# Loading the later x blocks of an attention and gated-MLP kernel through GpSimd's DMA queue

## The chip, the cores and the metric

The kernel runs on one core of a Trainium2 chip. The metric is the device time of one execution in microseconds (us), and the median of several executions is compared. A core has a matrix engine (TensorE, PE in the profile), three engines for elementwise work (VectorE DVE, ScalarE ACT, GpSimd POOL), a fifth, SyncE (SP), which here only issues transfers, and 16 DMA engines that move data between the chip's main memory (DRAM) and the on-chip memory. Each of the five engines has a queue of instructions of its own and works through it in order.

## The reference

For 2048 tokens of width 576, all in float32:

```python
xn = layernorm(x)                       # x: 1 x 2048 x 576
q, k, v = split(xn @ wqkv)              # 32 heads of 18
s = softmax(q @ k.T * 18**-0.5) @ v     # per head, over all 2048 keys
s = concat_heads(s) @ wo
gate = xn @ W_gate                      # 576 x 4608
h = where(gate > 0, gate, 0) * (xn @ W_up)
g = silu(h @ W_down)                    # 4608 x 576
out = x + s * g
```

## The kernel before

Every float32 product is made of three products of a high and a low part of its operands, so each operand is first split in two ("split", by GpSimd for the weights).

*First stage.* The 2048 tokens are normalized and transposed in four groups g of 512 tokens. Each group's x becomes nine chunks of 64 features (KC = 9), high and low part, and is kept as a tile `x` of 128 rows: rows 0 to 63 and rows 64 to 127 hold the same kind of chunk for the two row halves of TensorE. The groups are also written to DRAM as `xTd`, and q, k and v are made from them and written to DRAM (`qd`, `kd`, `vd`).

*Main stage.* 144 units (numbered k in the code), 36 for each group of 512 tokens. Unit k = 36 g + f makes 128 of the 4608 hidden features for group g: `up(k)` issues 54 matmuls `pg<-x,gw` (27 for each row half, three for each chunk of x, chunk 0 first), woven together with matmuls of attention (`pm` for the maxima of the scores, `psx` for the scores). After an odd unit TensorE does 64 matmuls `po` of attention, after an even one the down projections `py` of the two units before, which read `hh` (h, split) and `dw` (W_down, split).

*The x tiles.* There are eleven buffers (`xA`, KC + 2), nine of them in use. A takeover to the next group therefore runs like this: in `up(k)` of the last unit but one of a group (f = NF - 2, k = 34, 70 and 106), `load_x` is called for chunks 0 and 1 of the next group, into the two free buffers; in the last unit (k = 35, 71 and 107), after each chunk c of the old group has been read, `load_x` is called for chunk c + 2 of the new one. Each `load_x` issues two transfers of 64 rows x 4 KB (256 KB). So there are 4 and then 14 transfers at each of three takeovers; the first group is loaded in the same way at the end of the first stage.

*What sets the order.* The order on TensorE, VectorE and GpSimd is that of the code (kept by `pinned`, `mm`, `vec` and `gp`); the transfers on SyncE are partly kept in the code's order and partly ordered by a scheduler. A transfer on SyncE or GpSimd waits in its queue for the buffer to be free and for one of eight semaphores that the queue's transfers take in turn, so for the landing of the transfer eight before it; what is behind it in the queue waits too. The x loads have their own issuing line, L299 in the profile. GpSimd's other instructions all carry L85, and most of SyncE's L97, since helpers record them. On GpSimd stand, for each unit: the split of the next unit's weights `gw<-rg`, the split of `dw<-rd`, the low part of `hh`, and some adds into `y`.

Of the kernel before, what the change touches and what calls it, by code (L numbers as in the profile page):

```python
# [19 lines left out]
def kernel(  # L20
# [10 lines left out]
    nc = tc.nc  # L31
# [129 lines left out]
    def xtile(pl):  # L161
        return pl.tile([P, 2, 512], F32R, tag="x", name="x")
# [132 lines left out]
    def load_x(g, c):  # L295
        xc = xtile(xA)
        for t in range(2):
            pinned(
                nc.sync.dma_start(  # L299
                    xc[t * R : (t + 1) * R].rearrange("p a s -> p (a s)").bitcast(F32),  # L300
                    xTd[g, c // 2, c % 2 * R : c % 2 * R + R],
                )
            )
        xcur.setdefault(g, []).append(xc)

    with ExitStack() as st:
# [293 lines left out]
        for g in range(NQ):  # L600
# [64 lines left out]
            else:  # L665
                for j in range(4):
                    v_job(wv, g, j)
                    if j == 0 and g == 0:
                        nxt = load_rows(g + 2)
                    if j == 1:  # L670
                        spill(g, marks[-1] if g == 0 else None)
                    if j and g == NQ - 2:
                        for c in range(3 * j - 3, 3 * j):
                            load_x(0, c)
# [24 lines left out]
    def up(k):  # L699

        g, f = units[k]
        gw = gus.pop(k)
        if k < N1 and (k % 2 == 0 or k == N1 - 1):
            ps = [psO.tile([P, 512], F32, name="po"), shared("pg2")]
        else:
            ps = [bank("pg0"), bank("pg1")]
        last = f == NF - 1 and k + 1 < len(units)
        if f == NF - 2 and k + 2 < len(units):
            for c in range(2):
                load_x(units[k + 2][0], c)  # L710
        xg = xcur[g]

        def ops(t, c, i, j, rows):
            return gw[rows, i, c, :], xg[c][rows, j, :]

        def half(t):
            for n, _ in enumerate(row_half(ps[t], ops, t)):
                c = n // len(PRODUCTS)
                if t and last and n % len(PRODUCTS) == 2 and c + 2 < KC:
                    load_x(units[k + 1][0], c + 2)  # L720
                    if c == KC - 3:
                        load_up(k + 2)
                yield

        return ps, [half(t) for t in range(2)]
# [439 lines left out]
```

## Time and profile before

| | |
|---|---|
| median of 3 runs | 2573.6 us (2573.19 to 2574.91) |
| the profiled execution | 2572.87 us |
| its span | 2571.1 us |
| PE, busy | 2564.9 us |
| DVE, ACT, POOL, busy | 1847.1, 1474.5, 1274.7 us |
| transfers x<-xTd | 72, of 256 KB each, all on SyncE's queue |

The span reaches from the first to the last instruction of the profiled execution; the 1.8 us between it and that execution's time lie around it. Busy times of different engines lie beside each other and don't add up. Positions such as 681.18 are us from the span's start.

### The profile page before, as it was taken

The page shows a single profiled execution, that of the slowest core. Times are in us where ns is not written, and L with a number is a line of the kernel's source. Part 1 is how long each engine was busy: PE and PEld are TensorE (multiplying, and loading weights), DVE is VectorE, ACT ScalarE, POOL GpSimd, SP SyncE. Part 2 cuts the span into 40 slices and gives each one's busy share as a digit, 9 for nine tenths or more (in the row PEclk, how much of TensorE's full clock was granted, in tenths as well). Part 3 has the DMA queues.
Part 4 walks back from the last instruction along what each step waited for, and adds up shares of the span by engine and source line. Part 5 has one row for each costly group of instructions (what it writes and reads, how often), then busy time and mean ns, then how long its engine had stood idle before and what let it go on. Part 6 is the DMA issues. An engine that isn't in the chain of part 4 may idle for free.

```text
span 2571.1 us, 61531 instructions
## 1 busy us (share of the span) xinstructions
PE 2564.9 (100%) x25301; PEld 2035.3 (79%) x25301; DVE 1847.1 (72%) x3019; ACT 1474.5 (57%) x3005; POOL 1274.7 (50%) x1003
## 2 busy tenths in 40 slices
PE   9999999999999999999999999999999999999999
PEld 8899987777777777777777777777777777777788
DVE  6336677777877778877777777887777877778125
ACT  3222146666666666666666666666666666666652
POOL 5246764444464444444464444444445444444554
PEclk9999999999999999999999999999999999999999
DMA  8965432323543223222363322332354232222246
GB/s 255 298 205 134 103 86 47 85 68 81 125 112 71 72 70 72 64 71 70 93 145 81 74 71 69 73 77 58 80 130 108 69 79 69 70 62 59 68 137 200
DMA packets 263833, 254.60 MB, mean 99 GB/s; under 512 B 27648, under 2 KB 208640, under 8 KB 263552
## 3 DMA queue, kind: packets, MB, share of 16 engines
q1 hardware_dynamic: 255808, 223.01, 34.9%
q0 software_dynamic: 7744, 27.66, 3.2%
q8 instruction: 199, 3.26, 0.6%
q14 instruction: 82, 0.67, 0.1%
HBM read 203.54 MB, written 46.53 MB: 97 GB/s over the span
## 4 chain that ended last, share of the span: by engine, by line
PE 98%; DVE 1%; POOL 0%; issue 0%; DMA 0%; ACT 0%; POOLq 0%; ACTq 0%
PE pg L68 34%; PE po L68 18%; PE py L68 18%; PE pm L68 10%; PE psx L68 10%; PE pq L68 3%; PE pw L68 2%; PE pv L68 2%; PE tps L76 0%; PE warm L76 0%; DMA qd<-hh 0%; POOL gw L85 0%; DVE hh L129 0%; POOL kd L85 0%; POOL kq L85 0%
## 5 line engine op out<-in xcount | busy, mean ns | idle before, releaser
L268 DVE TENSOR_REDUCE mx<-pm 128x1 f32<-128x512 f32 x2048 | 1371.6, 690 | 355.7 <-PE pm L68 283.7
L68 PE MATMUL pg<-x,gw 64*128 64x512 f32 x7533 | 1359.3, 392 | 0.0
L97 ACT ACTIVATE p<-psx 128x512 f32<-128x512 f32 x2048 | 1097.8, 604 | 203.1 <-PE psx L68 162.7
L68 PEld LDWEIGHTS pg<-x,gw 64*128 64x128 f32 x7533 | 1027.4, 186 | 84.5 <-issue 1.8
L85 POOL TENSOR_TENSOR hh<-h,hh 128x512 fp32r<-128x512 f32 x144 | 185.3, 1287 | 810.1 <-ACT hh L740 810.0
L68 PE MATMUL py<-dw,hh 64*128 64x288 f32 x6912 | 477.7, 292 | 0.0
L68 PEld LDWEIGHTS py<-dw,hh 64*128 64x128 f32 x6912 | 472.8, 184 | 5.8 <-ACT h L97 0.6
L68 PE MATMUL po<-p,va 128*32 128x512 f32 x4096 | 452.7, 594 | 0.0
L68 PEld LDWEIGHTS po<-p,va 128*32 128x32 f32 x4096 | 126.5, 110 | 291.3 <-issue 280.1
L85 POOL TENSOR_TENSOR gw<-rg,gw 128x1152 fp32r<-128x1152 f32 x131 | 349.9, 2671 | 10.5
L790 DVE TENSOR_TENSOR y<-py,y 128x288 f32<-128x288 f32 x422 | 171.7, 452 | 139.7 <-PE py L68 139.6
L68 PE MATMUL psx<-qT,kq 56*128 56x512 f32 x608 | 231.0, 392 | 0.0
L68 PE MATMUL pm<-kq,qT 54*128 54x512 f32 x608 | 226.0, 396 | 0.0
L85 POOL TENSOR_TENSOR dw<-rd,dw 128x576 fp32r<-128x576 f32 x144 | 206.1, 1432 | 11.5
L68 PE MATMUL psx<-kq,kA 56*128 56x512 f32 x512 | 195.2, 393 | 0.0
L68 PE MATMUL psx<-kq 56*128 56x512 f32 x512 | 195.0, 393 | 0.0
L68 PE MATMUL pm<-kA,kq 54*128 54x512 f32 x512 | 191.7, 397 | 0.3 <-DVE mx L268 0.3
L68 PE MATMUL pm<-kq 54*128 54x512 f32 x512 | 191.3, 397 | 0.0
L774 ACT ACTIVATE mark<-ident 128x1 f32<-128x1 f32 x288 | 58.4, 203 | 219.2 <-PE py L68 219.0
L85 POOL CAST gw<-rg 128x1152 fp32r<-128x1152 f32 x131 | 153.8, 1174 | 57.3 <-DMA rg<-in_B_W_up_dram 51.0
L85 POOL TENSOR_TENSOR y<-add,y 128x576 f32<-128x576 f32 x61 | 87.3, 1431 | 186.3 <-ACT add L97 180.8
L740 ACT ACTIVATE hh<-h 128x512 fp32r<-128x512 f32 x144 | 90.8, 631 | 123.2 <-DVE h L733 123.2
(106 smaller groups left out, 2543.1 us busy)
## 6 DMA issues: line engine op xcount, KB each, us to landing
rd<-in_B_W_down_dram SPq DMA_DIRECT2D x144, 288.0 KB
rg<-in_B_W_gate_dram SPq DMA_DIRECT2D x131, 288.0 KB
rg<-in_B_W_up_dram SPq DMA_DIRECT2D x131, 288.0 KB
x<-xTd SPq DMA_DIRECT2D x72, 256.0 KB
qd<-hh POOLq DMA_DIRECT2D x16, 512.0 KB, 4.2
kd<-hh POOLq DMA_DIRECT2D x16, 512.0 KB, 5.7
xTd<-x SPq DMA_DIRECT2D x16, 512.0 KB
kq<-kd SPq DMA_DIRECT2D x210, 36.0 KB
```

What stands on the lines that cost most here:

```text
L68: return tc.keep_in_program_order(nc.tensor.matmul(*args, **kw))
L85: return lambda *args, **kw: tc.keep_in_program_order(op(*args, **kw))
L97: i = op(*args, **kw)
L268: vec(nc.vector.tensor_reduce(mx[:, h, b, j, c : c + 1], ps, axis=AX.X, op=ALU.max))
L740: copy = nc.scalar.activation(hhs[k][:, 0], h, AF.Copy)
L774: seen.append(pinned(nc.scalar.activation(mark, ident[:, :1], AF.Copy)))
L790: vec(nc.vector.tensor_tensor(ys[j][:, cs], outs_[m], ys[j][:, cs], ALU.add))
```

## The change

The x tiles of the first group are still issued by SyncE; those of the second, third and fourth group (g = 1, 2, 3) are issued by GpSimd.

```diff
@@ load_x(g, c)
         xc = xtile(xA)
         for t in range(2):
             pinned(
-                nc.sync.dma_start(
+                (nc.gpsimd if g else nc.sync).dma_start(
                     xc[t * R : (t + 1) * R].rearrange("p a s -> p (a s)").bitcast(F32),
                     xTd[g, c // 2, c % 2 * R : c % 2 * R + R],
                 )
```

54 of the 72 transfers change their queue. The orders on TensorE, VectorE and ScalarE stay as they are. Three places at the first takeover (units 34 to 36) show what moves; the other two takeovers have the same pattern.

GpSimd, units 34 and 35, after the change (`hh`, `gw`, `dw` and `y` are as above, `rg` and `rd` are the weights as loaded):

```order
L85 TENSOR_TENSOR gw<-rg,gw 128x1152
L299 DMA x<-xTd 64x1024 x4
L85 TENSOR_TENSOR hh<-h,hh 128x512
L85 TENSOR_TENSOR y<-add,y 128x576
L85 CAST dw<-rd 128x576
L85 TENSOR_TENSOR dw<-rd,dw 128x576
L85 CAST gw<-rg 128x1152
L85 TENSOR_TENSOR gw<-rg,gw 128x1152
L85 CAST dw<-rd 128x576
L85 TENSOR_TENSOR dw<-rd,dw 128x576
L299 DMA x<-xTd 64x1024 x14
L85 TENSOR_TENSOR hh<-h,hh 128x512
```

Before, the same rows stood there without the two of L299. The four transfers now stand between the split of unit 35's weights and hh of unit 34, the fourteen between the split of dw and hh of unit 35.

SyncE at the same place, before (`od<-on` writes attention's results, `kq<-qd` and `kA<-kd` load strips of q and k, `qT<-nr` the negated maxima):

```order
L97 DMA od<-on 18x512 x2
L299 DMA x<-xTd 64x1024 x4
L97 DMA rd<-in_B_W_down_dram 128x576
L299 DMA x<-xTd 64x1024 x14
L97 DMA rg<-in_B_W_gate_dram 64x9x128
L97 DMA rg<-in_B_W_up_dram 64x9x128
L97 DMA rd<-in_B_W_down_dram 128x576
L97 DMA kq<-qd 18x1024 x2
L97 DMA rg<-in_B_W_gate_dram 64x9x128
L97 DMA rg<-in_B_W_up_dram 64x9x128
```

and now:

```order
L97 DMA od<-on 18x512 x2
L97 DMA rd<-in_B_W_down_dram 128x576
L97 DMA rg<-in_B_W_gate_dram 64x9x128
L97 DMA rg<-in_B_W_up_dram 64x9x128
L97 DMA rd<-in_B_W_down_dram 128x576
L97 DMA kq<-qd 18x1024 x6
L97 DMA rg<-in_B_W_gate_dram 64x9x128
L97 DMA rg<-in_B_W_up_dram 64x9x128
```

The weights and the second rd no longer stand behind the x loads, and all six strips of q go together ahead of the following weights. At the second takeover six strips of k and the tile `va` of v move up in the same way.

TensorE, the end of unit 36's pg, where the last chunk (x_10348) is first read; the order is the same, and the two waits are now for GpSimd's transfers (DMASW) where they were for SyncE's (DMAHW). Before:

```order
L68 MATMUL pg0_10454<-x_10326,gw_10206 128x512
L68 MATMUL pg1_10455<-x_10348,gw_10206 128x512 [waits DMAHW0_49]
L68 MATMUL pg0_10454<-x_10348,gw_10206 128x512 [waits DMAHW7_49]
L68 MATMUL pg1_10455<-x_10348,gw_10206 128x512
L68 MATMUL pg0_10454<-x_10348,gw_10206 128x512
```

and now:

```order
L68 MATMUL pg0_10454<-x_10326,gw_10206 128x512
L68 MATMUL pg1_10455<-x_10348,gw_10206 128x512 [waits DMASW1_49]
L68 MATMUL pg0_10454<-x_10348,gw_10206 128x512 [waits DMASW0_49]
L68 MATMUL pg1_10455<-x_10348,gw_10206 128x512
L68 MATMUL pg0_10454<-x_10348,gw_10206 128x512
```

Each chunk has such a pair of waits, one for each row half.

## The prediction

> **What bounds the kernel now.** I read the page first: busy time, then the chain that ended last.
>
> ```profile
> span 2571.1 us, 61531 instructions
> PE 2564.9 (100%) x25301; PEld 2035.3 (79%) x25301; DVE 1847.1 (72%) x3019; ACT 1474.5 (57%) x3005; POOL 1274.7 (50%) x1003
> PE 98%; DVE 1%; POOL 0%; issue 0%; DMA 0%; ACT 0%; POOLq 0%; ACTq 0%
> ```
>
> TensorE is busy for 2564.9 of 2571.1 us and carries 98% of the chain. Its work is not touched, so the change can win at most the 6.2 us in which TensorE is idle in the whole span, and it loses whatever TensorE is made to wait. The question is only whether x still arrives in time. The execution that was profiled took 2572.87 us, 0.7 below the median of the runs, 2573.6; I make the sum as a difference and add it to the median.
>
> Next I read SyncE's queue in order of time where the second 512 tokens take over (units 34 to 36, k in the code). Columns: start, duration, instruction, count.
>
> ```profile
> 663.92 2.40 SPq L299 DMA_DIRECT2D x<-xTd  x4
> 680.72 0.36 SPq L97 DMA_DIRECT2D rd<-in_B_W_down_dram  x1
> 681.18 10.30 SPq L299 DMA_DIRECT2D x<-xTd  x14
> 692.22 0.63 SPq L97 DMA_DIRECT2D rg<-in_B_W_gate_dram  x1
> ```
>
> Four transfers (chunks 0 and 1) go early into free buffers. The other fourteen (chunks 2 to 8) go from 681.18 on, each pair when unit 35 has read a chunk for the last time; the next weights, rg, stand behind them. GpSimd in the same stretch, with its idle time before an instruction in brackets:
>
> ```profile
> 658.96 2.66 POOL L85 TENSOR_TENSOR gw<-rg,gw 128x1152 fp32r<-128x1152 f32 x1
> 672.76 1.28 POOL L85 TENSOR_TENSOR hh<-h,hh 128x512 fp32r<-128x512 f32 x1 [11.13 <-ACT hh L740]
> ...
> 685.23 1.43 POOL L85 TENSOR_TENSOR dw<-rd,dw 128x576 fp32r<-128x576 f32 x1
> 689.19 1.28 POOL L85 TENSOR_TENSOR hh<-h,hh 128x512 fp32r<-128x512 f32 x1 [2.53 <-ACT hh L740]
> 704.17 1.15 POOL L85 CAST gw<-rg 128x1152 fp32r<-128x1152 f32 x1 [13.70 <-DMA rg<-in_B_W_up_dram]
> ```
>
> GpSimd has the time. But its queue is in order, and the fourteen now stand behind the dw split, which ends at 685.23 + 1.43 = 686.66. Then TensorE, where unit 36, the first on the new tokens, stands:
>
> ```profile
> 686.28 7.07 PE L68 MATMUL po<-p,va 128*32 128x512 f32 x64
> 693.29 0.50 PE L68 MATMUL pg<-x,gw 64*128 64x512 f32 x1
> ...
> 702.26 0.64 PE L68 MATMUL pg<-x,gw 64*128 64x512 f32 x4
> 702.74 0.62 PE L68 MATMUL pg<-x,gw 64*128 64x512 f32 x3
> ```
>
> Unit 36 begins at 693.29. Its last six pg matmuls read chunk 8 and start at about 702.26; each chunk is read some 1.1 us after the one before. Last, the rate of the transfers (columns: stretch, length, busy time and count of PE, PEld, DVE, ACT, POOL, granted clock, DMA share, GB/s):
>
> ```profile
> 682.00:698.00 16.00, 16.00 (x142) 9.44 (x140) 10.52 (x18) 9.36 (x17) 5.86 (x4) 1.00 1.01 242
> 1290.00:1305.00 15.00, 15.00 (x134) 8.67 (x132) 9.55 (x16) 8.38 (x16) 4.94 (x4) 1.00 1.04 237
> 1897.00:1912.00 15.00, 15.00 (x134) 8.35 (x132) 9.51 (x17) 8.38 (x16) 5.09 (x4) 1.00 1.00 238
> ```
>
> In all three takeovers x moves at 237 to 242 GB/s with the DMA engines' share at 1.00 to 1.04. Fourteen transfers of 256 KB are 3.67 MB, so 15.2 to 15.5 us; before, they and the rd of 0.295 MB were through by about 681.18 + 0.8 + 3.96/0.242 = 698.4. TensorE needs two chunks in 2.2 us while a chunk takes 2.2 us to arrive, so the last chunk decides, with a slack of about 3 us after its landing.
>
> **The change part by part.** *Four early transfers.* They go at 658.96 + 2.66 = 661.62, into an idle time of 11.13 us. GpSimd's own issues in the trace, then the issue line of its 512 KB stores (KB, median us to landing), then a stretch in which little but such stores moves:
>
> ```profile
> 160.22 0.61 POOL L85 DMA_DIRECT2D qd<-hh  x1 [4.83 <-DVE hh L129]
> ...
> 162.02 0.60 POOL L85 DMA_DIRECT2D kd<-hh  x1
> ```
>
> ```profile
> qd<-hh POOLq DMA_DIRECT2D x16, 512.0 KB, 4.2
> ```
>
> ```profile
> 186.00:190.00 4.00, 3.91 (x51) 3.61 (x53) 3.64 (x7) 0.72 (x2) 3.92 (x3) 1.00 0.72 266
> ```
>
> The four issues around 160 move 256 KB each, as x does, at 0.61 us: 4 x 0.61 = 2.4 us, covered by the 11.13. Cost 0; without that cover hh would be 2.4 us late, and down projections read it much later.
>
> *Fourteen late transfers.* They start 686.66 - 681.18 = 5.48 us later than on SyncE, which is more than the slack. A 512 KB store lands 4.2 us after its issue (the issue line), of which 0.524/0.266 = 2.0 us are its bytes at the rate of the last row; so 2.2 us lie before and behind them. Chunk 8 lands at 686.66 + 2.2 + 15.2 = 704.1, if nothing else moves. Issue at 0.61 each would be done in 8.5 us and does not pace it. TensorE waits 704.1 - 702.26 = 1.8 us. The same for the third and fourth 512 tokens, from the end of dw and the activation h that ends the unit (at 703.46 here, 1.2 behind the first read of chunk 8):
>
> ```profile
> 703.46 0.60 ACT L97 ACTIVATE h<-pg 128x512 f32<-128x512 f32 x1 [0.35 <-PE pg L68]
> 1292.31 1.43 POOL L85 TENSOR_TENSOR dw<-rd,dw 128x576 fp32r<-128x576 f32 x1
> 1310.52 0.60 ACT L97 ACTIVATE h<-pg 128x512 f32<-128x512 f32 x1 [0.36 <-PE pg L68]
> 1899.47 1.43 POOL L85 TENSOR_TENSOR dw<-rd,dw 128x576 fp32r<-128x576 f32 x1
> 1917.68 0.60 ACT L97 ACTIVATE h<-pg 128x512 f32<-128x512 f32 x1 [0.36 <-PE pg L68]
> ```
>
> 1293.74 + 2.2 + 15.5 - 1309.32 = 2.1 us, and 1900.90 + 2.2 + 15.4 - 1916.48 = 2.0 us. Sum of the lower ends: 5.9 us.
>
> *SyncE's queue runs ahead.* With x gone from it, rg goes when gw is split (684.5), and rd and six strips of q go from 686.7 on, beside x instead of behind it; for the third 512 tokens also six strips of k and the tile va. That is new competition:
>
> ```profile
> rd<-in_B_W_down_dram SPq DMA_DIRECT2D x144, 288.0 KB
> kq<-qd SPq DMA_DIRECT2D x96, 72.0 KB
> kA<-kd SPq DMA_DIRECT2D x174, 36.0 KB
> va<-vd SPq DMA_DIRECT2D x16, 320.0 KB
> ```
>
> ```profile
> 717.60:719.60 2.00, 2.00 (x20) 1.68 (x18) 1.90 (x4) 1.89 (x4) 0.63 (x1) 1.00 0.47 127
> ```
>
> The last row is a stretch in which almost only such strips move: 127 GB/s, on about half of the engines. At most x loses rd 0.295/0.242 = 1.2 us and q 6 x 0.074/0.127 = 3.5 us at each takeover, 4.7; at the second also k 0.221/0.127 = 1.7 and va 0.328/0.242 = 1.4. Together 3 x 4.7 + 3.1 = 17.2 us; at least 0, if they fit beside x. The share of 1.01 says full; but these engines reached 415 GB/s in another stretch (row below), so 242 is not all they can do. I take half, 8.6 us.
>
> *GpSimd held up.* The issues wait for landings (one of eight semaphores each), so the last goes out when the sixth has landed, about 686.66 + 2.2 + 6 x 1.08 + 1 = 696 to 698. Then come hh of unit 35 (1.28 us; TensorE needs it 0.4 us into the py that follow unit 36) and gw of unit 37 (3.85 us, done by about 703; before, it started at 704.17 after waiting 13.70 for rg). Both earlier than needed: cost 0. If the cover went, hh would be late next. That rg comes sooner wins nothing, since TensorE did not wait for it.
>
> Sum: 5.9 + 8.6 = 14.5 us, with ends at 5.9 and 23.1. 2573.6 + 14.5 = 2588.1 us.
>
> *A rule against this.* The rate of GpSimd's queue for this load is in no row; the fastest stretch I found is SyncE storing 128-partition tiles:
>
> ```profile
> 64.00:67.00 3.00, 3.00 (x30) 2.72 (x28) 0.28 (x1) 0.20 (x1) 0.76 (x1) 1.00 1.03 415
> ```
>
> The Trainium skill's "DMA: Bandwidth & Descriptors", section "Anatomy of one DMA", fits a transfer from GpSimd as about 2.0 us plus its bytes at 436 GB/s. As an estimate by that page, the fourteen would land at 686.66 + 2.0 + 8.4 = 697.1 and TensorE would not wait at all: sum 0, the first rival. Against it, the Trainium skill's "SBUF — State Buffer", section "Door 1: The DMA port swizzle", says that 64 partitions reach only half of the ports; the 242 GB/s agree, and x still moves 64 partitions at a time.
>
> **The rivals.** *x arrives in time after all* (not slower): GpSimd's queue moves x faster, say because both halves of a chunk overlap better. It decides at the rate that moves 3.67 + 0.295 MB between 686.66 + 1.1 = 687.8 (half of the 2.2 on each side) and 702.26 - 1.1 = 701.2: 3.96/13.4 = 296 GB/s. For it speaks the 415; against it three stretches at 237 to 242 for this very transfer, and GpSimd's stores at 266. Then nothing is lost: 2573.6, at most 1 us off.
> *GpSimd keeps only two transfers in flight* (its queue too short): 7 x (2.2 + 2.16) = 30.5 us instead of 15.2, 15 us more at each takeover, 2588.1 + 45 = 2633. Against it: the four issues around 160 went out back to back at 0.6 us each with none landed.
> *Faster*: SyncE's freed queue takes waits off TensorE. It has 6.2 us of idle time in the whole span, and none in the stretches above, where its busy time is the full 16.00 and 15.00 us; 2568 at best.
>
> **How the numbers follow.** From no change, 0.2% is 5.1 us, about what a measurement of this kernel can tell. The forecast (late x, sum between the ends 5.9 and 23.1) has 0.75; x in time, or nearly so, 0.16; two in flight 0.05; faster 0.03; the remaining 0.01 goes with slower, for mishaps. Slower therefore 0.81, same 0.16, faster 0.03. The forecast's own range is 2579.5 to 2596.7. The range reaches down to 2575, into the case of x nearly in time, and up to 2598; it leaves out the two in flight and most of no wait at all.
>
> **What would show it.** The three groups of fourteen x issues on GpSimd start right behind dw at 686.7, 1293.7 + w and 1900.9 + w, where w is the delay gathered so far, and take 9 to 11 us each. TensorE waits for x three times, in pieces of about 1 us at the last chunks of units 36, 72 and 108, 3 to 8 us in each; the matmul counts and their mean times stay. The cast of gw no longer waits 13.7 us for rg. Fewer than 2 us of waits at each takeover would mean a faster queue or free competition; waits at py for hh or pg for gw, that GpSimd was held longer than I think.

## The result and the profile after

The changed kernel takes 2601.35 us (median of 5 runs, 2600.62 to 2602.84) against 2573.65 for the kernel before: 27.7 us more, ratio 1.0108 (95% interval 1.0097 to 1.012). It is slower, as forecast; the size, 14.5 us, was about half of what came, and 2601.35 lies above the range's end of 2598. The profiled execution of the changed kernel took 2601.35 us, its span is 2599.6.

The page, for the rows that answer to those of before:

```profile
span 2599.6 us, 61558 instructions
PE 2578.6 (99%) x25301; PEld 2040.9 (79%) x25301; DVE 1853.2 (71%) x3019; ACT 1475.7 (57%) x3005; POOL 1301.7 (50%) x1057
PE 96%; DMA 2%; DVE 1%; POOL 0%; issue 0%; ACT 0%; POOLq 0%; ACTq 0%
L68 PE MATMUL pg<-x,gw 64*128 64x512 f32 x7533 | 1371.7, 394 | 14.2 <-DMA x<-xTd 13.8
x<-xTd POOLq DMA_DIRECT2D x54, 256.0 KB, 9.8
```

TensorE's work is the same 25301 matmuls. Of the 28.5 us by which the span grew, 14.8 are idle time of TensorE (21.0 us now, 6.2 before) and 13.7 are more busy time (2578.6 against 2564.9). Before, the matmuls `pg<-x,gw` never waited:

```profile
L68 PE MATMUL pg<-x,gw 64*128 64x512 f32 x7533 | 1359.3, 392 | 0.0
```

Now TensorE sits idle 14.2 us ahead of them, 13.8 of these for x. The last row of the page has the 54 transfers of x, now on GpSimd's queue, with a median of 9.8 us from issue to landing.

The first takeover in order of time: SyncE's queue, then GpSimd's.

```profile
681.05 0.36 SPq L97 DMA_DIRECT2D rd<-in_B_W_down_dram  x1
684.91 0.60 SPq L97 DMA_DIRECT2D rg<-in_B_W_gate_dram  x1
685.56 0.63 SPq L97 DMA_DIRECT2D rg<-in_B_W_up_dram  x1
687.02 0.36 SPq L97 DMA_DIRECT2D rd<-in_B_W_down_dram  x1
687.44 2.83 SPq L97 DMA_DIRECT2D kq<-qd  x6
709.85 0.60 SPq L97 DMA_DIRECT2D rg<-in_B_W_gate_dram  x1
```

```profile
685.57 1.42 POOL L85 TENSOR_TENSOR dw<-rd,dw 128x576 fp32r<-128x576 f32 x1
686.94 4.10 POOL L299 DMA_DIRECT2D x<-xTd  x8
694.57 0.52 POOL L299 DMA_DIRECT2D x<-xTd  x1 [3.53 <-PE psx L68]
...
704.19 0.52 POOL L299 DMA_DIRECT2D x<-xTd  x1 [0.29 <-DMA x<-xTd]
704.72 1.29 POOL L85 TENSOR_TENSOR hh<-h,hh 128x512 fp32r<-128x512 f32 x1
705.95 1.14 POOL L85 CAST gw<-rg 128x1152 fp32r<-128x1152 f32 x1
```

The fourteen start right behind the dw split, as worked out (686.94 against 686.66). Ahead of x and beside it SyncE now sends rg, rd and six strips of q, which stood behind x before. Eight issues go out at once; the other six wait, five of them for a landing of x by these rows (the profile puts the first of the six down to a `psx` matmul), so the last leaves at 704.19. TensorE's weight loads that waited for x, with the wait in brackets, and the down projections that follow:

```profile
696.56 0.18 PEld L68 LDWEIGHTS pg<-x,gw 64*128 64x128 f32 x1 [0.56 <-DMA x<-xTd]
701.50 0.18 PEld L68 LDWEIGHTS pg<-x,gw 64*128 64x128 f32 x1 [4.17 <-DMA x<-xTd]
703.95 0.28 PEld L68 LDWEIGHTS pg<-x,gw 64*128 64x128 f32 x1 [0.80 <-DMA x<-xTd]
...
709.72 0.18 PEld L68 LDWEIGHTS pg<-x,gw 64*128 64x128 f32 x1 [1.03 <-DMA x<-xTd]
711.83 2.29 PEld L68 LDWEIGHTS py<-dw,hh 64*128 64x128 f32 x32
```

From here on a takeover is judged by its *lateness*: how much further the down projections `py` behind the first unit of the new tokens stand from a `po` group five units earlier (the one behind unit 31, at the first takeover) than they did before. For the first takeover the `po` rows (chain of waits, before and after) and the `py` row of before are

```profile
619.02 7.00 PE po L68 x64
```

```profile
619.32 7.00 PE po L68 x64
```

```profile
703.22 2.94 PEld L68 LDWEIGHTS py<-dw,hh 64*128 64x128 f32 x42
```

(711.83 - 619.32) - (703.22 - 619.02) = 8.31 us. In the same way the second takeover gives (1330.68 - 1234.75) - (1310.27 - 1226.10) = 11.76 and the third (1945.26 - 1853.65) - (1917.44 - 1833.25) = 7.42. The three make 27.5 of the 28.5 us of span. The waits alone don't: grouped over the run they are

```profile
PEld pg L68 <- DMA x<-xTd: 22.7, 18, 4.2
PE pg L68 <- DMA x<-xTd: 13.8, 9, 3.7
```

What is missing is in TensorE's clock, by stretch (length, busy time and count of PE, PEld, DVE, ACT, POOL, granted clock, DMA share, GB/s):

```profile
690.00:698.00 8.00, 7.64 (x65) 3.62 (x57) 3.40 (x5) 3.58 (x7) 2.07 (x5) 1.00 1.05 221
698.00:701.00 3.00, 0.00 (x0) 0.00 (x0) 0.05 (x1) 0.38 (x1) 0.52 (x1) 1.00 1.03 227
701.00:706.00 5.00, 4.32 (x20) 2.65 (x20) 1.93 (x3) 1.86 (x4) 2.83 (x5) 0.66 1.00 243
706.00:711.00 5.00, 3.94 (x30) 2.75 (x32) 2.64 (x5) 3.51 (x6) 4.14 (x5) 1.00 0.40 120
```

After the 4 us gap the granted clock is 0.66 on the mean of 5 us (0.50 in the middle), so matmuls count as busy for longer. The last wait, at 709.72, ends with a landing of x when the clock is back at 1.00: here x sets the end, and the slow clock fills time that would have been a wait.

### The profile page after: what moved, and what is told of

The parts are those of the page before. It is cut to its first block, busy times and chain, and to the rows that moved or that the text cites. A ratio compares the mean times of both kernels' runs of the same rounds, so it can differ in the third digit from the quotient of the medians.

```text
span 2599.6 us, 61558 instructions
## 1 busy us (share of the span) xinstructions
PE 2578.6 (99%) x25301; PEld 2040.9 (79%) x25301; DVE 1853.2 (71%) x3019; ACT 1475.7 (57%) x3005; POOL 1301.7 (50%) x1057
## 3 DMA queue, kind: packets, MB, share of 16 engines
q1 hardware_dynamic: 251488, 208.85, 32.5%
## 4 chain that ended last, share of the span: by engine, by line
PE 96%; DMA 2%; DVE 1%; POOL 0%; issue 0%; ACT 0%; POOLq 0%; ACTq 0%
PE pg L68 33%; PE py L68 18%; PE po L68 17%; PE pm L68 10%; PE psx L68 9%; PE pq L68 4%; DMA x<-xTd 2%; PE pw L68 2%; PE pv L68 2%; PE tps L76 0%; PE warm L76 0%; POOL dw L85 0%; POOL x L299 0%; DVE wqk L638 0%; DVE hh L129 0%
## 5 line engine op out<-in xcount | busy, mean ns | idle before, releaser
L68 PE MATMUL pg<-x,gw 64*128 64x512 f32 x7533 | 1371.7, 394 | 14.2 <-DMA x<-xTd 13.8
L85 POOL TENSOR_TENSOR dw<-rd,dw 128x576 fp32r<-128x576 f32 x144 | 205.9, 1430 | 11.5
```

The source lines that it names most:

```text
L68: return tc.keep_in_program_order(nc.tensor.matmul(*args, **kw))
L85: return lambda *args, **kw: tc.keep_in_program_order(op(*args, **kw))
```

## The experiments

Three readings of the loss were set against each other. *Shared*: one set of DMA engines serves both queues, and x is late by its place behind the dw split and by all that SyncE now sends ahead of it. *Queue*: GpSimd's queue moves x more slowly by itself. *Clock*: TensorE's slow stretches are the loss. The table has each run's three latenesses, from its own `po` and `py` rows as above, its median and its ratio to the kernel before (2573.6 to 2573.8 beside it). The latenesses are from one profiled execution each, and executions of one run lie up to 5 us apart (2592.10 to 2596.75 in pool_all_held, of which the slowest was profiled), and how much of that lies in the latenesses is not known, so a difference of a few us between two sums is safe only where it shows at each takeover.

| run | lateness at the three takeovers, us | sum | median, us | ratio (95%) |
|---|---|---|---|---|
| changed kernel | 8.3, 11.8, 7.4 | 27.5 | 2601.35 | 1.0108 (1.0097 to 1.012) |
| early_only | 0.0, 0.0, 0.0 | 0.0 | 2573.64 | 0.9999 (0.999 to 1.0008) |
| pool_all_held | 2.8, 3.1, 3.0 | 8.9 | 2593.18 | 1.008 (1.0064 to 1.0095) |
| pool_strips_held | 4.6, 6.1, 4.8 | 15.4 | 2589.05 | 1.0059 (1.0044 to 1.0074) |
| pool_weights_held | 3.7, 7.2, 3.8 | 14.7 | 2592.11 | 1.0069 (1.0053 to 1.0086) |
| sync_held | 3.6, 4.5, 3.7 | 11.8 | 2589.1 | 1.0061 (1.0046 to 1.0076) |
| sync_weights_first | 5.6, 5.1, 6.5 | 17.2 | 2590.54 | 1.0066 (1.0049 to 1.0083) |
| x_first | 4.0, 2.1, 5.1 (gw, not x) | 11.2 | 2582.88 | 1.0038 (1.0023 to 1.0053) |
| strips_beside | 5.7, 8.7, 6.3 | 20.6 | 2601.28 | 1.0107 (1.0092 to 1.0122) |
| weights_beside | 6.9, 7.3, 6.7 | 20.8 | 2595.49 | 1.0084 (1.0069 to 1.0099) |
| all_beside | 11.9, 13.8, 11.5 | 37.1 | 2610.35 | 1.014 (1.0123 to 1.0157) |

**early_only**: of the kernel before, only the four early transfers go to GpSimd.

```diff
-                nc.sync.dma_start(
+                (nc.gpsimd if g and c < 2 else nc.sync).dma_start(
```

> The kernel before with only the four early x transfers of each block (chunks 0 and 1) through GpSimd, and the fourteen late ones through SyncE. The prediction's term for the early four is nothing: 2573.6 us (2572.5 to 2575). Queue: the same, as they are issued some 25 us before they are needed. A loss here would show that the early part had a price.

No loss. All of it is in the fourteen late transfers.

**pool_all_held**: the changed kernel, with the transfers that ran ahead held back. `hold[0]` is the last x transfer of a takeover, from its issue until unit f = 3 of the new tokens; `after(i, j)` lets i wait for the end of j. Each of rg, rd ("w"), the q and k strips and va ("s") passes through `hold_back`.

```diff
+    HELD = 'ws'
...
+    def hold_back(i, kind):
+        if hold[0] is not None and kind in HELD:
+            after(i, hold[0])
...
-            sp.dma_start(rds[k], wd[f * P : (f + 1) * P, :])
+            hold_back(sp.dma_start(rds[k], wd[f * P : (f + 1) * P, :]), "w")
```

> The changed kernel, x through GpSimd, with one addition: SyncE's transfers that ran ahead at a takeover (rg, rd, the q and k strips, va) wait until the last of the sixteen x transfers has landed. Shared: only the later place of x is left, about 2579.5 us (2577 to 2583). Queue: GpSimd's queue is as slow as before, so about 2600 us (above 2595).

(The last of the x transfers is the fourteenth, not the sixteenth.) The total missed both ranges. The lateness points to *shared*: 8.9 of the 27.5 us are left, so 18.6 came from what SyncE sent. The queues by themselves, in the kernel before, in this one, and in the changed one, each over a stretch full of x (packets, MB, share of the 16 engines; q1 is SyncE's queue, q0 GpSimd's):

```profile
DMA packets 996, 3.30 MB, mean 236 GB/s; under 512 B 195, under 2 KB 195, under 8 KB 993
q1 hardware_dynamic: 993, 3.27, 101.7%
```

```profile
DMA packets 993, 3.26 MB, mean 233 GB/s; under 512 B 202, under 2 KB 202, under 8 KB 990
q0 software_dynamic: 990, 3.23, 103.5%
```

```profile
DMA packets 720, 2.21 MB, mean 221 GB/s; under 512 B 157, under 2 KB 157, under 8 KB 718
q0 software_dynamic: 484, 1.61, 75.9%
q1 hardware_dynamic: 234, 0.58, 27.1%
```

Alone, GpSimd's queue moved 3.23 MB in 14 us (690 to 704), SyncE's 3.27 in 14 us (684 to 698): 231 and 234 GB/s, the same packets filling the same engines. In the changed kernel (690 to 700) x got 1.61 MB in 10 us, 161 GB/s, because SyncE's packets took 27.1% of the engines' time. That falsifies *queue* and shows *shared*. The Trainium skill's "DMA: Bandwidth & Descriptors", section "Queues, rings and completion order", says that each DMA engine takes turns between the queues that have work for it. The trace agrees in so far as both queues had their part of the same engines, 75.9% and 27.1%; the turns themselves it does not show.

The total was worse than expected because the held rg came late in its turn (SyncE's issue of rg, then GpSimd's cast of gw):

```profile
706.32 0.60 SPq L97 DMA_DIRECT2D rg<-in_B_W_gate_dram  x1
```

```profile
711.92 1.15 POOL L85 CAST gw<-rg 128x1152 fp32r<-128x1152 f32 x1 [12.39 <-DMA rg<-in_B_W_up_dram]
```

TensorE then waited for gw (1.64 us at 715.84) and for ScalarE's `p` behind the `py`, which the expectation had left out. So for runs that hold something back the lateness, not the total, tells what x lost.

**pool_strips_held** and **pool_weights_held**: the same with `HELD = 's'` and `HELD = 'w'`.

> The changed kernel, with only the q and k strips and va of a takeover held until the last x transfer has landed; rg and rd still run ahead. Shared: the later place (2 us) and rg and rd (some 2.7 us) are left at each of three takeovers, about 2588 us (2585 to 2591). Queue: about 2600 us.

> The changed kernel, with only rg and rd of a takeover held until the last x transfer has landed; the q and k strips and va still run ahead. Shared: the later place (2 us), the strips (3.5 us) and at the second takeover k and va (3 us) are left, about 2593 us (2589 to 2596). Queue: about 2600 us.

Both came near *shared* and 8 to 12 us below *queue*. For pool_weights_held that is in part luck: its parts had promised 19.5 us of lateness, 14.7 came, and the held rg, late in its turn, added about 6 elsewhere. And measured so, the pieces do not add up: over the 8.9 of the place, rg and rd cost 6.5 and the strips with va 5.8, and 6.3 of the 27.5 are missing. The three runs at the end are on that.

**sync_held** and **sync_weights_first**: GpSimd issues no x. In the first, SyncE's late x waits for the dw split, GpSimd's place; in the second, rg and rd are put ahead of x. The lines with `kept` keep these transfers in the code's order.

```diff
+            if g and c == 2 and t == 0:
+                after(ld, dw_end[0])
...
+                        kept, sp.kept = sp.kept, True
                         load_up(k + 2)
+                        sp.kept = kept
```

```diff
-                    if c == KC - 3:
-                        load_up(k + 2)
...
+        if units[k][1] == NF - 1 and k + 1 < len(units):
+            kept, sp.kept = sp.kept, True
+            load_up(k + 2)
+            load_down(k + 1)
+            sp.kept = kept
```

> SyncE issues every x again, as before the change, but its first of the fourteen late x transfers of a takeover waits until GpSimd has ended the last dw split, which is where GpSimd's queue has them; rg and rd stay behind x. Theory "shared" (one set of DMA engines; x is late by its place and by what SyncE now sends ahead of it): only the later place is left, about 2 us at each of three takeovers as the prediction worked out, so about 2579.5 us. Rival "queue" (GpSimd's queue moves x more slowly by itself): the queue's share of the 27.7 us is gone and the place's is left, again some 6 us, so about 2579.5 too; but if the late start itself were the cause, this run would stand near 2601. Rival "clock" (the granted TensorE clock drops after a gap and that drop is most of the loss): with small gaps no drop, 2579 or less.

> The kernel before, all x through SyncE, with the takeover's rg and rd transfers put ahead of the fourteen late x transfers in SyncE's queue; GpSimd issues no x. Shared: x is late by the time that rg and rd take on the DMA engines, and by what SyncE waits for a free rg buffer: 3 to 5 us a takeover, 2583 to 2588 us. Queue: SyncE's queue is fast, x at most 2 us late, 2574 to 2579.5 us.

Without GpSimd's queue the same loss appears: 11.8 us of lateness from the place alone (8.9 on GpSimd) and 17.2 with rg and rd ahead (15.4 for place, rg and rd on GpSimd). Both totals are above their forecasts, by some 10 and by 2.5 us. That SyncE's runs come out later does not show a better queue: in sync_held rg, rd and two strips follow x so closely (699.40 to 704.17) that they run beside its last part, and in pool_all_held nothing does. Of the 17.3 us by which sync_held's span is longer than before, 5.5 lie outside the three latenesses; TensorE's waits for ScalarE's `p` grew there by 3.1 us over the run (4.8 against 1.7), and the rest stays open.

**x_first**: the changed kernel, but in the last unit of a group GpSimd issues the fourteen ahead of its gw and dw splits.

```diff
                     if c == KC - 3:
+                        split_up(k + 1)
+                        split_down(k)
                         load_up(k + 2)
...
+        early_split = k >= len(units) - 1 or units[k][1] < NF - 1
+        if early_split:
+            split_up(k + 1)
...
+            if k in rds and early_split:
                 split_down(k)
```

> The changed kernel, but in the last unit of a block of 512 tokens GpSimd issues the fourteen x transfers ahead of its splits of gw and dw (both splits moved behind them, ahead of the next rg load), so that x starts as soon as its buffers come free, ahead of what SyncE sends. Shared: x has the engines almost alone again and lands in time, about 2573.6 us (2572 to 2577; the splits of gw and dw come some us later and are needed later still). Queue: the same transfers by the same queue, still late by the queue's slowness, 2580 us or more.

x was in time: all waits of TensorE for it come to 0.3 us over the three takeovers, with the strips still running beside it. So the queue can do the job from the old place, at least where rg comes behind x (at 696.86). The total, 2582.88, missed *shared* and lies where *queue* had put it, but for another reason: gw is needed right at the takeover, not later as the expectation assumed. TensorE's waits for gw at the first and second takeover, and the six us that hold each wait and the six after (columns as above):

```profile
696.89 0.19 PEld L68 LDWEIGHTS pg<-x,gw 64*128 64x128 f32 x2 [2.00 <-POOL gw L85]
1307.38 0.19 PEld L68 LDWEIGHTS pg<-x,gw 64*128 64x128 f32 x2 [2.01 <-POOL gw L85]
```

```profile
692.00:698.00 6.00, 4.42 (x35) 2.02 (x29) 1.03 (x2) 1.30 (x3) 5.53 (x6) 1.00 1.06 227
698.00:704.00 6.00, 6.00 (x42) 4.93 (x40) 4.23 (x7) 4.47 (x9) 2.19 (x2) 0.72 1.07 231
...
1303.00:1309.00 6.00, 4.42 (x39) 2.16 (x33) 1.53 (x3) 1.80 (x4) 5.83 (x5) 1.00 1.06 221
1309.00:1315.00 6.00, 6.00 (x55) 5.89 (x53) 5.33 (x9) 5.79 (x12) 1.71 (x2) 1.00 1.06 219
```

This is the test of *clock*. The two waits are alike, but after the first the clock was 0.72 on the mean of 6 us, a loss of 6 x 0.28 = 1.7 us, and after the second 1.00. The latenesses are 3.99 and 2.09: the drop cost 1.9 us of its own, because nothing else was late behind it. So the clock is a real price where work is ready again. In the changed kernel it is not what decides: the last wait of each takeover still ends with a landing of x (709.72, 1329.38, 1944.38), at the first and third with the clock back at 1.00. At the second the clock came back just then, so there the two cannot be told apart by the last 0.2 us.

**strips_beside**, **weights_beside**, **all_beside**: on the missing 6.3 us. In the changed kernel rg goes at 684.91, x at 686.94; so rg has two us in which little else moves (from 687 to 690 SyncE's queue still had 110.8% of the engines' time and x 3.7%). Where the weights are held, the strips have that time (685.29 in pool_weights_held, 687.44 in the changed kernel). Each of the two runs used the same gap once. In these runs what is not held waits for the dw split, so that it runs beside x:

```diff
+        elif hold[0] is not None and kind in BESIDE:
+            after(i, gate[0])
```

`gate[0]` is that dw split. The three have the weights held and the strips beside, the other way round, and all beside.

> As the run that holds rg and rd until x has landed, but the q and k strips and va of a takeover may not start before the dw split ends, which is when x starts on GpSimd, so they run beside x and not in the two idle us ahead of it. Theory "gap" (the pieces measured apart summed to 21 of 27.5 us because each of them could use the idle time ahead of x): the strips cost x their full price beside it, so TensorE ends the up projection of the takeover 4.6 to 6.3 us late at the first and third (3.65 and 3.84 where the strips started early) and 8.5 to 10 at the second (7.21); with the later gw of that run some 5 us more elsewhere: 2596 to 2600 us. Rival "pair" (strips and weights cost more only where both run at once): as before this change, 3.7, 7.2 and 3.8, about 2592 us.

> As the run that holds the strips and va until x has landed, but rg may not start before the dw split ends, so rg and rd run beside x. Gap: their 0.59 and 0.295 MB at 0.242 MB/us, 3.7 us, on top of the later place (2.8 to 3.1): 6.5 us at each takeover in place of 4.5, 6.1 and 4.8, about 2593 us. Pair: no change from that run, about 2589 us.

> The changed kernel with one addition: rg of a takeover may not start before the dw split ends, so that everything SyncE sends runs beside x. Gap: what rg moved in the idle time ahead of x (about 2 us a takeover) now costs x time: 2605 to 2608 us. Pair: all of it ran at once already, so about 2601 us.

*Gap* is borne out: without the early start the strips and va cost 11.7 us over the place (5.8 with it), rg and rd 11.9 (6.5 with it), and all together 28.2 (18.6 in the changed kernel), each of them more at all three takeovers. The totals lie 1 to 3 us above their forecasts. Of all_beside, SyncE's queue at the first takeover and the queues' shares from 690 to 704:

```profile
687.98 0.60 SPq L97 DMA_DIRECT2D rg<-in_B_W_gate_dram  x1
688.63 0.63 SPq L97 DMA_DIRECT2D rg<-in_B_W_up_dram  x1
689.36 0.59 SPq L97 DMA_DIRECT2D rd<-in_B_W_down_dram  x1
690.00 3.35 SPq L97 DMA_DIRECT2D kq<-qd  x6
```

```profile
q0 software_dynamic: 606, 1.96, 64.1%
q1 hardware_dynamic: 1422, 1.16, 42.6%
```

rg goes two us later than in the changed kernel (687.98 against 684.91, of which 1.0 is the run's own offset), and x is down to 1.96 MB in 14 us, 140 GB/s, against 3.23 MB in the same stretch of pool_all_held. So the gap is worth 5.9 us by the strips and 5.4 by the weights, and the 6.3 us that were missing are this gap, counted in both runs that held something back: 8.9 + 11.7 + 11.9 less one gap are 26.6 to 27.1 of the 27.5.

*Pair* is not wholly out: without the gap 8.9 + 11.7 + 11.9 = 32.5, and 37.1 were measured in all_beside. These 4.6 us may be more, since in strips_beside up to 1.7 us of the third takeover's lateness is the clock's, after the last wait for x. But in all_beside there is also a newcomer: the weights of the unit after next, which in strips_beside and weights_beside go out only after the last wait for x. At the first takeover SyncE's issue of them, TensorE's last wait for x, and SyncE's share of the engines from 710.5 to 715.3:

```profile
710.54 0.60 SPq L97 DMA_DIRECT2D rg<-in_B_W_gate_dram  x1
```

```profile
715.34 0.30 PEld L68 LDWEIGHTS pg<-x,gw 64*128 64x128 f32 x4 [0.69 <-DMA x<-xTd]
```

```profile
q1 hardware_dynamic: 1020, 0.51, 56.0%
```

The other two takeovers have the same order (rg at 1329.69 and 1949.77, last waits at 1335.81 and 1954.47). A late x thus meets the next weights too. That this is the 4.6 us is argued, not shown: no run holds those weights back.

## Why the prediction was wrong in size

- *TensorE bounds the kernel and can win nothing.* Right: it has 96% of the chain, and no run is faster than the kernel before.
- *The four early transfers cost 0.* Right, by early_only.
- *The fourteen come later by their place, 5.9 us.* Right mechanism, too small: 8.9 in pool_all_held. The transfers took 706.32 - 687.69 = 18.6 us there (first issue on GpSimd at 687.69; SyncE's rg, which waited for the last landing, at 706.32) where 2.2 + 15.2 = 17.4 were put: about 1 us at each takeover.
- *SyncE's queue runs ahead: rd, q, k and va at half their price, 8.6 us.* **This step failed.** What SyncE sends cost x 18.6 us. Two errors are in it. First, the working names rg among what goes early and then gives it no price, while 0.59 MB at 0.242 MB/us are 2.4 us a takeover, 7.3 in all; rg and rd together cost 11.9 us when they run beside x. Second, half was chosen because another stretch had reached 415 GB/s. But the DMA share beside x already read 1.00 to 1.04, and that was the row to believe: with full engines, what one queue gets the other loses. Strips and va cost 11.7 us beside x, against an upper end of 3 x 3.5 + 3.1 = 13.6. That these two are so near is in part luck: the 3.5 us for six strips of q came from a stretch that used about half of the engines, and in strips_beside the six took 9.7% of the engines over 20.1 us, or 1.95 us. What the prediction had no term for is the gap ahead of x, which gave 5.4 to 5.9 us back.
- *Issues in 8.5 us, the last at 696 to 698, hh and gw in time.* The issues took until 704.71, 17.8 us, since their landings paced them and these were late; the cost was still 0: hh at 704.72 and gw at 705.95 held up nobody, and gw waited for no rg.
- *The rivals.* "x in time" needed 296 GB/s; x had 161, and alone 231. The fit with 436 GB/s that the Trainium skill's "DMA: Bandwidth & Descriptors", section "Anatomy of one DMA", gives for GpSimd does not hold for these tiles of 64 partitions: 231 GB/s in pool_all_held. "Two in flight" is out: eight issues left in 4.10 us. "Faster" is out.
- *What would show it.* Waits in pieces of about 1 us were foreseen; there was one of 3.4 to 4.2 us at each takeover as well, and behind it the slow clock, which the prediction did not mention and which makes the page's 13.8 us of waits read as half of the real loss. The mean time of `pg<-x,gw` did not stay either: 394 ns against 392.

## To carry to other kernels

When a transfer moves from one queue to another, list first what stood behind it in the old queue: that is now ahead of it, and where the DMA share beside it is already 1.0, what it moves takes that engine time from the transfer that moved, less only what fits into an idle gap ahead of it. A second queue adds no bandwidth here; it removes an order, and the order of the kernel before (x first, weights and strips behind) was what kept x in time. Judge the loss by how late a fixed group of work comes, not by the waits that the page lists, since a slowed clock books part of it as busy time.

## What the hardware showed beyond that

TensorE's granted clock fell to 0.50 at gaps of 1.6 to 3.7 us in the changed kernel and x_first, for about 3.4 us or a multiple of it: once 3.4 us at the changed kernel's first takeover, four times that at the second, twice at the third. In x_first a stretch with 1.58 us of idle time (6.00 - 4.42) brought it down at one takeover and a stretch with the same 1.58 us did not at the next, so the length of the gap alone does not decide. The Trainium skill's "TensorE: Matmul & The Clock Gate", section "What's actually happening", has the clock fall after an idle window of about 3.4 us that runs freely; as an estimate by that page, one such window at half clock costs 1.7 us, as after the first wait in x_first. But there the idle time ahead of the drop, 1.58 us, was shorter than the window.
